# First mixture of the fused kernel: rows normalized on VectorE tile by tile ahead of their transposes, side products in the second layers

## The chip, the cores and the metric

One core of a Trainium2 chip runs the whole program. The metric is the device time of one execution in microseconds (us), as the median of several runs. A difference of 0.5% (5.3 us) is about the smallest that a measurement of this kernel can tell from none.

## The reference, cut to what matters

Three stages follow each other: a linear attention, a mixture of experts with a gate per row, and a second mixture with a capacity per expert.

```python
def _attn_ref(q, k, v, g_norm):                    # (8, 8, 576, 64) each
    kv = np.einsum('bhsd,bhse->bhde', k, v)
    out = np.einsum('bhsd,bhde->bhse', q, kv)
    rms = np.sqrt(np.mean(out * out, axis=-1, keepdims=True) + 1e-06)
    return out / rms * g_norm
def _moe_ref(x, expert_emb, tau, w1, w2):          # x (4608, 512), 8 experts, F = 1024
    logits = xn @ en.T / tau                       # xn, en: rows over their norms
    expert_idx = np.argmax(logits, axis=1)
    gate_w = probs[np.arange(N), expert_idx]       # probs: softmax of the logits
    for e in range(E):
        mask = expert_idx == e
        out[mask] = gate_w[mask, None] * (np.maximum(x[mask] @ w1[e], 0.0) @ w2[e])
def _moe2_ref(x, w_gate, w1, w2):                  # at most 576 rows an expert, best logits first
    ...
        out[mask] = np.maximum(x[mask] @ w1[e], 0.0) @ w2[e]
```

The division by `rms` and the product with `g_norm` at the end of the attention are what the change moves.

## The kernel before, in words

**The stages.** The attention loop takes the heads in 40 steps. It stores rows of 528 numbers in DRAM (`xbuf`): 512 values not yet normalized, 8 gate logits, and 8 factors 1/rms, one a head. Rows of one expert are then gathered by an index table, one tile of up to 128 rows at a time. An expert has five such tiles (`TL`), in two pieces: columns 0 to 255 and the rest (0 to 319 and the rest for expert 0). The products of a piece are laid out with the features on the partitions, so each tile is turned before it is used.

**One tile.** `gather` (L667) issues the indirect DMAs of an expert's tiles on GpSimd (L675) and then, on the same engine, `normed` for each (L661): L664 multiplies the 128 x 512 values by the row's factors and L665 by `g_norm`, in place. These two are called a pair here. `xtile` (L685) turns the tile on TensorE (L695), ScalarE writes the upper half `xh` (L697), VectorE the rest `xl` (L698), and `gate_in` (L627) reads the tile for the gates: a sum of squares on ScalarE (L630) and a copy of eight logits on GpSimd (L631). Five `xg` buffers exist.

**One expert.** Numbers are split in two for the products: `layer1` (L710) does three matmuls in place of one (L724 to L726), for a quarter f of the 1024 features and one piece c. Then ScalarE writes `hh` (L732) and VectorE `hl` (L733) out of PSUM. `layer2_t` (L742) does the second layer in two halves `dp`, with L763 to L765, and ScalarE copies the result to `yT` (L773). `rows_out` (L817) turns the results back, ScalarE scales them by the gate `gts` into `yr` (L790), VectorE copies the row index beside them (L791), and `rows_l` makes the logits of the second mixture (L810 to L814). PSUM has two buffers for products (`mm`) and two for turned tiles (`tp`).

**Weights.** `wcast` (L566) takes the next 128 x 1024 block: ScalarE's L578 writes `whi`, VectorE's L584 the rest `wlo` from the raw block, and SP then issues a further load into one of three raw buffers (L562).

**Gates and side products.** `gates(e)` is a generator of small VectorE operations on 128 x 5 and 128 x 40 (L639 to L656); `next` runs a part, `run_gen` the rest. `w2g_ops` (L833) makes a product of two weight matrices that the last experts use: ScalarE lays out `wgB` (`big`, L854), and then 128 VectorE operations L861 on 128 x 512, one for each call of `aside`.

**The order of the work** is the order in which this code is written: each engine has one queue and takes its instructions in that order, SP and GpSimd for their DMAs too. `ASIDE` says how many asides stand in each of five places of an expert's loop, and `XT0` the steps of the last attention group at which expert 0's first three tiles are turned. Expert 0 is written out by hand (L1070 to L1091), experts 1 to 5 are a loop (L1423), experts 6 and 7 follow by hand. In expert 0's second piece, expert 1's tiles are gathered; in each loop those of the next expert. The loop before:

```python
            for c in range(2):
                layer1(0, e, f, c)
                aside(ASIDE[0])
                if f > 1:
                    next(gt, None)
...
                if f < 2 or 2 * (f - 2) + c < 3:
                    wcast()
            if f == 1:
                gather(0, e + 1)
        wcast()
        layer2_t(e, 0, 0)
        xtiles(0, e + 1, 0, 1)
        aside(ASIDE[1])
        layer2_t(e, 0, 1)
        xtiles(0, e + 1, 1, 3)
        aside(ASIDE[2])
```

Of the kernel before, what the change touches and what calls it, by code (L numbers as in the profile page):

```python
# [36 lines left out]

NWARM = (18, 28, 6)

ASIDE = (1, 5, 5, 5, 3)  # L40

EARLY = 0

# [18 lines left out]

NYR = 4

XT0 = (5, 6, 8)

ROWS = (4.4, 2.8, 1.6)

# [12 lines left out]
def fused_kernel(ctx, tc, q, k, v, g_norm, emb, tau, w1, w2, wgate, v1, v2, out):  # L81
    nc = tc.nc
    V = nc.vector
# [16 lines left out]
    early = ExitStack()  # L100
# [125 lines left out]
    def run_gen(g):  # L226
        for _ in g:
            pass
# [432 lines left out]
    def normed(xg, n, eng):  # L661

        x = xg[:n, :HD].rearrange("p (h d) -> p h d", h=H)
        eng.tensor_tensor(x, x, xg[:n, HD + E:XP, None].to_broadcast([n, H, D]), op=OP.mult)  # L664
        eng.tensor_tensor(x, x, gB[:n, None, :].to_broadcast([n, H, D]), op=OP.mult)  # L665

    def gather(m, e, lo=0, hi=5, early=False, eng=nc.gpsimd):  # L667
        for i, (c, t, p, n, o) in list(enumerate(TL[m, e]))[lo:hi]:
            n += p
            if early:  # L670
                xg = mk(wpB, [128, XP], F32, "xg0", bufs=2) if i < 2 else kvx[0].rearrange("p a b c w -> p (a b c w)")[:, :XP]
            else:
                xg = mk(mp, [128, XP], F32, "xg", bufs=5)
            buf, idx, wd = (xbuf[:GA * TG * 128] if early else xbuf, tabi, XP) if m == 0 else (ybuf, tab2, YP)
            nc.gpsimd.indirect_dma_start(  # L675
                out=xg[:n, :wd], out_offset=None, in_=buf[:, :],
                in_offset=bass.IndirectOffsetOnAxis(ap=idx[:n, e * SC + t:e * SC + t + 1], axis=0))
            XG[m, e, i] = xg
        if m == 0 and eng:
            for i, (c, t, p, n, o) in list(enumerate(TL[m, e]))[lo:hi]:  # L680
                normed(XG[m, e, i], p + n, eng)

    XT = {}

# [22 lines left out]
    def layer1(m, e, f, c):  # L707
        run_gen(layer1_g(m, e, f, c))
# [33 lines left out]
    def layer2_t(e, c, dp, mid=None):  # L742
        run_gen(layer2_g(e, c, dp, mid))
# [205 lines left out]
    for n, st in enumerate(steps):  # L949
        gi, u, hg = st  # L950
        i = n % len(UNITS)
        if gi + 1 < NG and i in KVAT[gi > 0]:
            bg.append(kv(2 * gi + 2 + KVAT[gi > 0].index(i)))
        if n + 2 < len(steps):
            qa(*steps[n + 2])
        if i % 2 == 0 and i < 8:
            m = 4 * gi + i // 2 + 4
            if m < 2 * B:
                load_main(m // 2, "q", m % 2)
        if i == 9 and gi + 1 < NG:  # L960
            load_tail(gi + 1, "q")
        if gi == NG - 1 and i in XT0:
            xtile(0, 0, XT0.index(i), False)
        late = qb(*st, late)
        if i == 0 and gi > 0:
            bg.append(group_end(gi - 1))
        pump()
        if n in LOADS:
            wload(LOADS[n])
        if n in CASTS and n < 30:  # L970
            wcast(1, nc.gpsimd if CASTS[n] else V, 0)
        if gi == NG - 1:
            if i == 0:
                kvs.close()
                wpB = ctx.enter_context(tc.tile_pool(name="wpB", bufs=RING // 2))
                mo0 = ExitStack()
                MP["xh1"] = MP["xl1"] = mo0.enter_context(tc.tile_pool(name="moex", bufs=1))
                WP.append(wpB)
            elif n in CASTS:
                wcast(1, nc.gpsimd if CASTS[n] else V, 1)  # L980
            if i == EARLY:
                index(0, 3)
                gather(0, 0, 0, 3, early=True, eng=None)
            if i == SCALE:
                rows0 = [XG[0, 0, t] for t in range(2)]
                for t in range(2):
                    normed(rows0[t], 128, nc.gpsimd)
            if i == SCALE + 1:
                normed(XG[0, 0, 2], CUT - 256, V)
            if i == LASTP[0]:  # L990
                ge = group_end(gi)
            if i in LASTP:
                next(ge)
        if gi == 0 and i < 4:
            pump()
# [29 lines left out]
    while bg:  # L1025
        pump()
    index(2, NCOL)
    gather(0, 0, 3, 6, eng=None)
    LSUB[0](V)
    pe(1.1)  # L1030
    LSUB[1](V)
# [2 lines left out]
    for i, us in enumerate(ROWS):  # L1034
        pe(total - us - done)
        done = total - us
        normed(XG[0, 0, 3 + i], sum(TL[0, 0][3 + i][2:4]), V)
        xtiles(0, 0, 3 + i, 4 + i)
    run_gen(f0)
    grp.close()  # L1040
# [29 lines left out]
    gt = gates(0)  # L1070
    aside(1)
    for f in range(4):
        layer1(0, 0, f, 1)
        wcast()
        aside(1)
        if f == 0:
            next(gt)
            gather(0, 1)
        elif f < 3:
            next(gt)  # L1080
        else:
            run_gen(gt)
            ro = rows_out(0, 0)
            next(ro)
            next(ro)
    layer2_t(0, 1, 0, lambda: (run_gen(ro), xtiles(0, 1, 0, 1)))
    xtiles(0, 1, 1, 2)
    aside(2)
    layer2_t(0, 1, 1, lambda: xtiles(0, 1, 2, 3))
    xtiles(0, 1, 3, 5)  # L1090
    aside(2)  # L1091

# [330 lines left out]
    for e in range(1, E - ND):  # L1423
        gt = gates(e)
        if e == 2:
            flags()
        for f in range(4):
            for c in range(2):
                layer1(0, e, f, c)
                aside(ASIDE[0])  # L1430
                if f > 1:
                    next(gt, None)
                if f == 0:
                    if c == 0:
                        ro = rows_out(e - 1, 1)
                        next(ro)
                        next(ro)
                    else:
                        run_gen(ro)
                if f < 2 or 2 * (f - 2) + c < 3:  # L1440
                    wcast()
            if f == 1:
                gather(0, e + 1)
        wcast()
        layer2_t(e, 0, 0)
        xtiles(0, e + 1, 0, 1)
        aside(ASIDE[1])
        layer2_t(e, 0, 1)
        xtiles(0, e + 1, 1, 3)
        aside(ASIDE[2])  # L1450
        layer2_t(e, 1, 0)
        run_gen(rows_out(e, 0))
        xtiles(0, e + 1, 3, 5)
        aside(ASIDE[3])
        layer2_t(e, 1, 1)
        aside(ASIDE[4])


    e6, e7 = E - 2, E - 1
    for f in range(4):  # L1460
        layer1(0, e6, f, 0)
        if f == 0:
            gt = gates(e6)
        next(gt, None)
        if f == 0:
            ro = rows_out(e6 - 1, 1)
            next(ro)
            next(ro)
        if f == 1:
            run_gen(ro)  # L1470
        wcast()
        if f == 1:
            gather(0, e7)
    run_gen(wg)
    for f in range(4):
        layer1(0, e6, f, 1)
        wcast()
        if f in (1, 2):
            xtiles(0, e7, f - 1, f)
    H7.append(mk(mp, [128, KF, CAP[E - 1]], F32, "big"))  # L1480
    layer1(0, e7, 0, 0)
    a = logits_w(e6, 0)
    xtiles(0, e7, 2, 3)
    a()
# [713 lines left out]
```

## Time and profile before

| | us |
|---|---|
| median of 3 runs (lowest, highest) | 1067.63 (1066.28, 1070.65) |
| the profiled execution: its time, its span | 1072.25, 1070.5 |
| TensorE (PE) busy | 1020.1, 95% of the span |
| VectorE (DVE) busy | 732.2, 68% |
| ScalarE (ACT) busy | 526.8, 49% |
| GpSimd (POOL) busy | 293.5, 27% |

All rows are of one execution. A busy share is a mean over the whole span, and the stages differ: the first product of expert 0 starts near 137 us, that of expert 1 near 210 us, each further expert some 60 us later, and the last copy of L773 starts at 637 us; the second mixture follows. So a stretch is read by itself. Times within the program are counted from the start of the span. `PEclk` is the share of full speed that TensorE's clock was granted.

### The profile page before, as it was taken

Reading aid. Unit: us, or ns where it says so; the run is one execution under the profiler, and the core shown is the slowest. Engines: PE = TensorE matmul, PEld = TensorE weight load, DVE = VectorE, ACT = ScalarE, POOL = GpSimd, SP = SyncE. Lnnn points to the kernel's source line nnn. Section 1 sums busy time; section 2 is a strip of 40 time slices with the busy share of each in tenths; the row PEclk is TensorE's granted clock in tenths of the full one; section 3 lists DMA queues with packets and bytes.
Section 4 is the critical chain, followed back from the end, with each engine's and each line's share of the span. In section 5 each row is a group of like instructions: output and inputs, shape, how many; then the busy total and the mean of one; then the engine's idle time right before and its main releaser. Section 6 shows DMA issues by size and latency. Waiting matters only on the chain. (4 is left out here: it accounts for less than half of the span.)

```text
span 1070.5 us, 20601 instructions
## 1 busy us (share of the span) xinstructions
PE 1020.1 (95%) x8234; PEld 939.0 (88%) x8234; DVE 732.2 (68%) x1443; ACT 526.8 (49%) x915; POOL 293.5 (27%) x389
## 2 busy tenths in 40 slices
PE   7888798889999999999999998999999999999998
PEld 7777688789999999999988987989889898989896
DVE  4467876376978778786756765668685959595860
ACT  2566724754444545353643312556565656555551
POOL 2011427241616061423400113131304131313211
PEclk8999789889999999999999999999999999999999
DMA  9999535444343525243411114434334343424211
GB/s 285 379 346 326 190 138 189 156 134 145 119 139 98 163 95 167 86 158 108 139 47 59 41 47 141 149 109 157 120 129 159 110 148 118 149 99 152 106 55 45
DMA packets 94679, 152.46 MB, mean 142 GB/s; under 512 B 11321, under 2 KB 52281, under 8 KB 94579
## 3 DMA queue, kind: packets, MB, share of 16 engines
q1 hardware_dynamic: 85011, 121.65, 34.2%
q0 software_dynamic: 9040, 28.93, 8.4%
q8 instruction: 65, 1.06, 0.4%
q10 hardware_dynamic: 528, 0.52, 0.2%
q14 instruction: 35, 0.29, 0.1%
HBM read 121.26 MB, written 29.82 MB: 141 GB/s over the span
## 5 line engine op out<-in xcount | busy, mean ns | idle before, releaser
L724 PE MATMUL mm<-xh,whi 128*128 128x256 f32 (+7 forms) x512 | 156.2, 305 | 6.5 <-DVE hl L733 6.1
L763 PE MATMUL mm<-hh,whi 128*128 128x256 f32 (+7 forms) x512 | 156.4, 305 | 1.7 <-ACT hh L732 1.7
L725 PE MATMUL mm<-xl,whi 128*128 128x256 f32 (+7 forms) x512 | 153.2, 299 | 2.0 <-DVE xl L698 2.0
L726 PE MATMUL mm<-xh,wlo 128*128 128x256 f32 (+7 forms) x512 | 153.2, 299 | 0.0
L764 PE MATMUL mm<-hl,whi 128*128 128x256 f32 (+7 forms) x512 | 151.9, 297 | 1.0 <-DVE hl L1546 0.6
L765 PE MATMUL mm<-hh,wlo 128*128 128x256 f32 (+7 forms) x512 | 151.5, 296 | 0.0
L861 DVE SCALAR_TENSOR_TENSOR rc<-xg,big 128x512 bf16<-128x512 f32 x128 | 110.7, 865 | 2.6
L584 DVE TENSOR_TENSOR wlo<-wraw,whi 128x1024 fp32r<-128x1024 f32 x72 | 91.1, 1269 | 22.5 <-ACT whi L578 21.9
L724 PEld LDWEIGHTS mm<-xh,whi 128*128 128x128 f32 x512 | 98.2, 192 | 8.7 <-DVE hl L733 7.2
L725 PEld LDWEIGHTS mm<-xl,whi 128*128 128x128 f32 x512 | 98.3, 192 | 2.2 <-DVE xl L698 2.2
L763 PEld LDWEIGHTS mm<-hh,whi 128*128 128x128 f32 x512 | 96.9, 189 | 3.8 <-ACT hh L732 2.0
L726 PEld LDWEIGHTS mm<-xh,wlo 128*128 128x128 f32 x512 | 98.2, 192 | 0.0
L764 PEld LDWEIGHTS mm<-hl,whi 128*128 128x128 f32 x512 | 96.9, 189 | 1.4 <-DVE hl L1546 0.8
L765 PEld LDWEIGHTS mm<-hh,wlo 128*128 128x128 f32 x512 | 96.8, 189 | 0.0
L773 ACT COPY yT<-mm 128x512 f32<-128x512 f32 (+7 forms) x31 | 19.9, 643 | 149.9 <-PE mm L765 149.9
L675 POOL DMA_INDIRECT xg<-xbuf,tabi x40 | 43.5, 1088 | 171.8 <-ACT sj L630 74.9
L2097 POOL DMA_INDIRECT out<-tm,ti x40 | 43.7, 1092 | 160.2 <-ACT tm L2095 140.5
L578 ACT CAST whi<-wraw 128x1024 fp32r<-128x1024 f32 x72 | 74.9, 1044 | 0.4 <-DMA wraw<-in_moe_w 0.3
L732 ACT ACTIVATE hh<-mm 128x512 fp32r<-128x512 f32 (+7 forms) x56 | 36.8, 658 | 74.8 <-PE mm L726 72.1
L1840 DVE TENSOR_TENSOR wlo<-wraw,whi 128x1024 fp32r<-128x1024 f32 (+1 forms) x63 | 61.0, 987 | 11.6 <-ACT whi L1843 11.6
L665 POOL TENSOR_TENSOR xg<-xg,gB 128x512 f32<-128x512 f32 (+6 forms) x37 | 61.0, 1649 | 2.9
L733 DVE SCALAR_TENSOR_TENSOR hl<-mm,hh 128x512 fp32r<-128x512 f32 (+7 forms) x56 | 42.6, 760 | 21.6 <-ACT hh L732 21.5
(363 smaller groups left out, 2687.9 us busy)
## 6 DMA issues: line engine op xcount, KB each, us to landing
wraw<-in_moe_w SPq DMA_DIRECT2D x127, 512.0 KB, 3.9
kmain<-in_k SPq DMA_DIRECT2D x16, 576.0 KB, 8.7
vmain<-in_v SPq DMA_DIRECT2D x16, 576.0 KB, 11.0
xbuf<-xo SPq DMA_DIRECT2D x16, 528.0 KB, 11.5
qmain<-in_q SPq DMA_DIRECT2D x16, 512.0 KB, 9.8
ybuf<-yr SPq DMA_DIRECT2D x31, 260.0 KB, 2.1
xg<-in_moe_w SPq DMA_DIRECT2D x16, 256.0 KB
xg<-in_moe_w_gate SPq DMA_DIRECT2D x8, 256.0 KB, 3.8
```

Source lines behind the costliest of these rows:

```text
L578: nc.scalar.copy(hi, raw)
L584: eng.tensor_tensor(lo, raw, hi.bitcast(F32), op=OP.subtract)
L665: eng.tensor_tensor(x, x, gB[:n, None, :].to_broadcast([n, H, D]), op=OP.mult)
L724: nc.tensor.matmul(o, a, xh[:, kd, :N], start=(kd == 0), stop=False)
L725: nc.tensor.matmul(o, a, xl[:, kd, :N], start=False, stop=False)
L726: nc.tensor.matmul(o, b, xh[:, kd, :N], start=False, stop=(kd == KD - 1))
L763: nc.tensor.matmul(o, a, hh[:, kf, :N], start=(kf == 0), stop=False)
L764: nc.tensor.matmul(o, a, hl[:, kf, :N], start=False, stop=False)
L765: nc.tensor.matmul(o, b, hh[:, kf, :N], start=False, stop=(kf == KF - 1))
L861: V.scalar_tensor_tensor(junk, raws[i], 1.0, wgB[:, x], op0=OP.mult, op1=OP.mult, accum_out=w2g[:, i // KF, i % KF, x:x + 1])
L1840: V.tensor_tensor(l, x, h.bitcast(F32), op=OP.subtract)
L2097: st_ = nc.gpsimd.indirect_dma_start(out=out, out_offset=bass.IndirectOffsetOnAxis(ap=TI[e, t][:n, :1], axis=0), in_=yo[:n], in_offset=Non ...
```

## The change

- The pairs of experts 1 to 7 (35 tiles) leave `gather` and GpSimd. `gather` puts each tile into a queue `NQ`, and `norm(k)` runs `normed` on VectorE for the next k tiles; the calls stand one by one where the tile is wanted later. Expert 0's last three tiles were on VectorE before and now go by the same queue; its first two stay on GpSimd.
- In experts 1 to 5, the pairs stand after both products of the fourth quarter, after `layer2_t(e, 0, 0)` and its transposes, and two after `layer2_t(e, 0, 1)`. The aside after each product of the fourth quarter is left out; `ASIDE` has one more in each of two later places, so that a loop still has 26.
- Expert 0's second piece: the gates are finished ahead of the fourth quarter's product, and the logits and the first tile of `rows_out` come ahead of the last weight cast and aside there, not behind them.
- The third tile of expert 0 is turned one step of the attention loop earlier (`XT0`).

Below lines of the changed file are shifted: 664 and 665 are the same, L698 is L703, L733 is L738, L791 is L796, L675 is L681, L861 is L866.

```diff
-ASIDE = (1, 5, 5, 5, 3)
+ASIDE = (1, 5, 6, 6, 3)
...
-XT0 = (5, 6, 8)
+XT0 = (5, 6, 7)
...
-    def gather(m, e, lo=0, hi=5, early=False, eng=nc.gpsimd):
+    NQ = []
+
+    def norm(k=1):
+        for _ in range(k):
+            normed(*NQ.pop(0), V)
+
+    def gather(m, e, lo=0, hi=5, early=False):
...
             XG[m, e, i] = xg
-        if m == 0 and eng:
-            for i, (c, t, p, n, o) in list(enumerate(TL[m, e]))[lo:hi]:
-                normed(XG[m, e, i], p + n, eng)
+            if m == 0 and not early:
+                NQ.append((xg, n))
...
     gt = gates(0)
     aside(1)
     for f in range(4):
+        if f == 3:
+            run_gen(gt)
         layer1(0, 0, f, 1)
+        if f == 3:
+            ro = rows_out(0, 0)
+            next(ro)
+            next(ro)
         wcast()
         aside(1)
         if f == 0:
...
         elif f < 3:
             next(gt)
-        else:
-            run_gen(gt)
-            ro = rows_out(0, 0)
-            next(ro)
-            next(ro)
-    layer2_t(0, 1, 0, lambda: (run_gen(ro), xtiles(0, 1, 0, 1)))
+        if f > 1:
+            norm()
+    layer2_t(0, 1, 0, lambda: (run_gen(ro), xtiles(0, 1, 0, 1), norm()))
     xtiles(0, 1, 1, 2)
+    norm()
     aside(2)
-    layer2_t(0, 1, 1, lambda: xtiles(0, 1, 2, 3))
+    layer2_t(0, 1, 1, lambda: (norm(), xtiles(0, 1, 2, 3)))
...
                 layer1(0, e, f, c)
-                aside(ASIDE[0])
+                if f < 3:
+                    aside(ASIDE[0])
...
                     wcast()
+                if f == 3:
+                    norm()
             if f == 1:
                 gather(0, e + 1)
         wcast()
         layer2_t(e, 0, 0)
         xtiles(0, e + 1, 0, 1)
+        norm()
         aside(ASIDE[1])
         layer2_t(e, 0, 1)
+        norm(2)
         xtiles(0, e + 1, 1, 3)
...
             gather(0, e7)
+    norm()
     run_gen(wg)
     for f in range(4):
         layer1(0, e6, f, 1)
         wcast()
+        if f != 1:
+            norm()
         if f in (1, 2):
             xtiles(0, e7, f - 1, f)
...
     layer1(0, e7, 0, 0)
+    norm()
```

How this moves instructions, engine by engine (name of what is written, `<-` what is read, and the shape):

VectorE, expert 0's second piece, from the third quarter's `wlo` to the first row indices of `rows_out`, before:

```order
L584 TENSOR_TENSOR wlo_2617<-wraw_2328,whi_2616 128x1024
L649 TENSOR_SCALAR gw_2524<-gw_2524 128x5
L650 RECIPROCAL gw_2524<-gw_2524 128x5
L651 TENSOR_TENSOR gx_2528<-gx_2528,gw_2524 128x40
L733 SCALAR_TENSOR_TENSOR hl0_2487<-mm_2629,hh0_2486 128x576
L584 TENSOR_TENSOR wlo_2657<-wraw_2519,whi_2656 128x1024
L654 TENSOR_REDUCE gts_180<-gx_2528 128x5
L655 TENSOR_SCALAR gts_180<-gts_180 128x5
L656 RECIPROCAL gts_180<-gts_180 128x5
L791 COPY yr_2680<-tabi_178 128x8
L791 COPY yr_2689<-tabi_178 128x8
```

and in the change (`hl0_2487` of L738 is the last quarter's, as that of L733 above):

```order
L584 TENSOR_TENSOR wlo_2607<-wraw_2328,whi_2606 128x1024
L649 TENSOR_SCALAR gw_2524<-gw_2524 128x5
L650 RECIPROCAL gw_2524<-gw_2524 128x5
L651 TENSOR_TENSOR gx_2528<-gx_2528,gw_2524 128x40
L664 TENSOR_TENSOR xg_2530<-xg_2530 128x512
L665 TENSOR_TENSOR xg_2530<-xg_2530,gB_96 128x512
L654 TENSOR_REDUCE gts_180<-gx_2528 128x5
L655 TENSOR_SCALAR gts_180<-gts_180 128x5
L656 RECIPROCAL gts_180<-gts_180 128x5
L738 SCALAR_TENSOR_TENSOR hl0_2487<-mm_2624,hh0_2486 128x576
L796 COPY yr_2663<-tabi_178 128x8
L796 COPY yr_2672<-tabi_178 128x8
```

A pair of expert 1's first tile and the three operations that finish the gates now stand ahead of the last `hl`; the last `wlo` has gone from behind that `hl` to behind the two row indices.

VectorE, end of expert 1's first layer and start of its second (`xg_3088` to `xg_3092` are expert 2's tiles), before:

```order
L584 TENSOR_TENSOR wlo_3218<-wraw_3086,whi_3217 128x1024
L733 SCALAR_TENSOR_TENSOR hl1_2960<-mm_3223,hh1_2959 128x2x280
L861 SCALAR_TENSOR_TENSOR rc_2483,w2g_2482<-xg0_2926,big_2481 128x512
L654 TENSOR_REDUCE gts_180<-gx_3140 128x5
L655 TENSOR_SCALAR gts_180<-gts_180 128x5
L656 RECIPROCAL gts_180<-gts_180 128x5
L584 TENSOR_TENSOR wlo_3255<-wraw_3146,whi_3254 128x1024
L698 TENSOR_TENSOR xl0_3312<-tp_3313,xh0_3311 128x4x128
L861 SCALAR_TENSOR_TENSOR rc_2483,w2g_2482<-xg0_2926,big_2481 128x512
```

and in the change:

```order
L584 TENSOR_TENSOR wlo_3207<-wraw_3086,whi_3206 128x1024
L664 TENSOR_TENSOR xg_3088<-xg_3088 128x512
L665 TENSOR_TENSOR xg_3088<-xg_3088,gB_96 128x512
L738 SCALAR_TENSOR_TENSOR hl1_2960<-mm_3214,hh1_2959 128x2x280
L654 TENSOR_REDUCE gts_180<-gx_3130 128x5
L655 TENSOR_SCALAR gts_180<-gts_180 128x5
L656 RECIPROCAL gts_180<-gts_180 128x5
L664 TENSOR_TENSOR xg_3090<-xg_3090 128x512
L665 TENSOR_TENSOR xg_3090<-xg_3090,gB_96 128x512
L584 TENSOR_TENSOR wlo_3247<-wraw_3136,whi_3246 128x1024
L703 TENSOR_TENSOR xl0_3304<-tp_3305,xh0_3303 128x4x128
L664 TENSOR_TENSOR xg_3092<-xg_3092 128x512
```

The first tile's pair stands ahead of the last `hl`, the second ahead of the last `wlo`, and the aside L861 behind that `hl` is gone.

GpSimd, the gather of expert 2, before:

```order
L675 DMA xg_3094<-xbuf_71,tabi_178 128x528
L675 DMA xg_3096<-xbuf_71,tabi_178 80x528
L664 TENSOR_TENSOR xg_3088<-xg_3088 128x512
L665 TENSOR_TENSOR xg_3088<-xg_3088,gB_96 128x512
L664 TENSOR_TENSOR xg_3090<-xg_3090 128x512
```

and in the change:

```order
L681 DMA xg_3094<-xbuf_71,tabi_178 128x528
L681 DMA xg_3096<-xbuf_71,tabi_178 80x528
L631 COPY gvl_181<-xg_3088 128x8
L631 COPY gvl_181<-xg_3090 128x8
L631 COPY gvl_181<-xg_3092 128x8
```

The ten operations of the five pairs are gone from behind the DMAs, and the copies of the logits follow at once.

## Rows read from the trace of the kernel before

**Rows 1.** Table of stretches: us, PE, PEld, DVE, ACT, POOL busy, clock, DMA share, GB/s.

```profile
250.00:550.00 300.00, 298.40 (x2310) 286.66 (x2309) 227.43 (x492) 142.53 (x243) 105.48 (x100) 1.00 0.39 126
```

**Rows 2.** TensorE's waits, 176 to 300 us: total, times, longest, in us.

```profile
PE mm L724 <- DVE hl L733: 6.1, 3, 4.8
PE mm L763 <- ACT hh L732: 1.7, 1, 1.7
PE tp L784 <- ACT yr L790: 1.6, 1, 1.6
PE mm L764 <- DVE hl L733: 0.4, 1, 0.4
```

**Rows 3.** Table of stretches, columns as in rows 1.

```profile
160.00:190.00 30.00, 27.24 (x201) 25.59 (x200) 18.98 (x31) 13.48 (x22) 22.95 (x30) 1.00 0.57 181
193.30:200.00 6.70, 5.07 (x23) 4.57 (x23) 2.97 (x14) 4.10 (x8) 0.55 (x1) 0.50 0.68 231
229.30:234.20 4.90, 4.81 (x22) 4.81 (x23) 4.18 (x8) 0.00 (x0) 0.00 (x0) 0.50 0.67 218
234.20:240.00 5.80, 5.80 (x49) 5.80 (x48) 3.80 (x9) 4.52 (x6) 0.69 (x5) 1.00 0.27 91
```

**Rows 4.** VectorE by line, 177 to 189 us: busy us, mean ns, idle before.

```profile
L584 DVE TENSOR_TENSOR wlo<-wraw,whi 128x1024 fp32r<-128x1024 f32 x3 | 5.4, 1794 | 0.2 <-ACT whi L578 0.2
L643 DVE TENSOR_TENSOR gx<-gvl,gw 128x40 f32<-128x40 f32 x1 | 1.3, 1260 | 0.0
L646 DVE TENSOR_TENSOR gw<-gvn,gw 128x5 f32<-128x5 f32 x1 | 1.0, 1045 | 0.0
```

**Rows 5.** One line's instructions, whole run: min/median/max ns, first and last start.

```profile
L861 DVE SCALAR_TENSOR_TENSOR rc<-xg,big x128: 671/691/1861, 221.0 to 508.8; 128x512 bf16<-128x512 f32 x128
L584 DVE TENSOR_TENSOR wlo<-wraw,whi x72: 1199/1222/2111, 98.7 to 682.6; 128x1024 fp32r<-128x1024 f32 x72
L813 DVE TENSOR_TENSOR lr<-lr,gts x26: 153/174/1242, 197.3 to 578.8; 128x16 f32<-128x16 f32 x15, 64x8 f32<-64x8 f32 x3, 24x8 f32<-24x8 f32 x2, 128x8 f32<-128x8 f32 x1
L733 DVE SCALAR_TENSOR_TENSOR hl<-mm,hh x56: 668/740/874, 145.2 to 538.6; 128x512 fp32r<-128x512 f32 x24, 128x640 fp32r<-128x640 f32 x8, 128x576 fp32r<-128x576 f32 x4, 128x560 fp32r<-128x560 f32 x4
L665 DVE TENSOR_TENSOR xg<-xg,gB x3: 686/691/745, 162.3 to 169.4; 128x512 f32<-128x512 f32 x2, 96x512 f32<-96x512 f32 x1
```

**Rows 6.** VectorE by line, 217 to 229 us, columns as in rows 4.

```profile
L584 DVE TENSOR_TENSOR wlo<-wraw,whi 128x1024 fp32r<-128x1024 f32 x2 | 3.3, 1647 | 1.2 <-ACT whi L578 1.2
L813 DVE TENSOR_TENSOR lr<-lr,gts 128x8 f32<-128x8 f32 (+2 forms) x3 | 2.5, 834 | 0.1
L791 DVE COPY yr<-tabi 128x8 int32<-128x8 int32 (+2 forms) x3 | 1.8, 613 | 0.0
L814 DVE TENSOR_TENSOR L<-lr,vneg 128x8 f32<-128x8 f32 (+2 forms) x3 | 1.3, 429 | 0.1
L861 DVE SCALAR_TENSOR_TENSOR rc<-xg,big 128x512 bf16<-128x512 f32 x1 | 1.1, 1134 | 0.0
```

**Rows 7.** GpSimd by line, 213.5 to 226.9 us.

```profile
L665 POOL TENSOR_TENSOR xg<-xg,gB 128x512 f32<-128x512 f32 (+1 forms) x5 | 7.3, 1463 | 0.4
L664 POOL TENSOR_TENSOR xg<-xg 128x512 f32<-128x512 f32 (+1 forms) x5 | 5.7, 1136 | 0.0
```

**Rows 8.** GpSimd by line, 250 to 550 us.

```profile
L675 POOL DMA_INDIRECT xg<-xbuf,tabi x25 | 28.1, 1125 | 139.6 <-ACT xh L697 62.3 <-ACT sj L630 59.2 <-issue 18.2
```

**Rows 9.** ScalarE in order of time: start, us, then the idle time before.

```profile
188.45 1.21 ACT L854 COPY big<-xg 128x512 f32<-128x512 f32 x1 [2.09 <-DMA xg<-in_moe_w_gate]
```

**Rows 10.** VectorE by line, 250 to 550 us.

```profile
L861 DVE SCALAR_TENSOR_TENSOR rc<-xg,big 128x512 bf16<-128x512 f32 x121 | 105.5, 871 | 2.6
L698 DVE TENSOR_TENSOR xl<-tp,xh 128x512 fp32r<-128x512 f32 (+5 forms) x28 | 18.3, 653 | 28.0 <-ACT xh L697 28.0
```

**Rows 11.** TensorE and VectorE in order of time, near 137 us.

```profile
137.01 0.63 PE L725 MATMUL mm<-xl,whi 128*128 128x320 f32 x1 [2.02 <-DVE xl L698]
...
136.09 0.53 DVE L522 TENSOR_TENSOR oh<-iob,sf 128x360 bf16<-128x360 bf16 x1
```

More of the change, by code (lines that the diff above doesn't have):

```diff
@@ L982, in fused_kernel @@
                 index(0, 3)
-                gather(0, 0, 0, 3, early=True, eng=None)
+                gather(0, 0, 0, 3, early=True)
             if i == SCALE:
@@ L1027, in fused_kernel @@
     index(2, NCOL)
-    gather(0, 0, 3, 6, eng=None)
+    gather(0, 0, 3, 6)
     LSUB[0](V)
@@ L1036, in fused_kernel @@
         done = total - us
-        normed(XG[0, 0, 3 + i], sum(TL[0, 0][3 + i][2:4]), V)
+        norm()
         xtiles(0, 0, 3 + i, 4 + i)
@@ L1481, in fused_kernel @@
     layer1(0, e7, 0, 0)
+    norm()
     a = logits_w(e6, 0)
```

## The prediction

> **What bounds the kernel now.** I read the table of stretches first. From 250 to 550 us, where most of the loops of experts 1 to 5 run and 25 of the 35 moved tiles are gathered, TensorE is busy 298.4 of 300 us at the full clock and VectorE 227 of 300 [rows 1]. Whatever leaves or joins another engine there can give back 1.6 us at most; it can only cost, if VectorE becomes late. So I looked for places where TensorE does wait. The list of its waits from 176 to 300 us, where expert 0 ends and expert 1 runs, has 6.1 us for `hl` on VectorE in three waits, the longest 4.8 (it ends at 229.4 us), 0.4 for the same tile under another line, 1.7 for `hh` and 1.6 for `yr` on ScalarE: 9.8 us [rows 2]. The waits between 190 and 197 us and the one that ends at 229.4 are each followed by a stretch in which the granted clock is 0.50, that is 1.2 in place of 2.4 GHz: 193.3 to 200 and 229.3 to 234.2 us. Shorter waits need not bring that: from 160 to 190 us TensorE is busy 27.2 of 30 us and the clock is 1.00 throughout [rows 3].
>
> Next, why VectorE is late there. From 177 to 189 us its small operations last six times as long as elsewhere: the five-element L646 takes 1.0 us, the forty-element L643 1.26, against a median of 0.17 for the small L813; three `wlo` take 1.79 each, against 1.22 [rows 4, 5]. From 217 to 229 us it is the same [rows 6]. Both stretches are those in which GpSimd runs its pairs L664 and L665, five tiles each time; the second string lies between 213.5 and 226.9 us [rows 7]. Operations that read SBUF twice are the ones stretched most clearly: L861 takes 671 ns at least, 691 as a median and 1861 at most; `hl`, which reads PSUM, never passes 874 over all its widths [rows 5]. I read it as the two engines holding each other up in SBUF, one instruction at a time.
>
> **The change, part by part.**
>
> (a) Pairs off GpSimd. 35 tiles lose L664 and L665 there (1.1 and 1.5 us each [rows 7]). What stands behind them on GpSimd is not in a hurry: from 250 to 550 us it sat idle for 140 us ahead of its gathers [rows 8]. By itself this part is worth 0. What counts is that the stretching of VectorE ends.
>
> In the stretch before 229.4 us it makes: two L584 of mean 1647 against 1222, 0.85; three L813 by 0.66 and three L791 by 0.45 over 0.17, 3.3; three L814 by 0.26, 0.8; one L861 by 0.44: 5.4 us [rows 5, 6]. They all stand in one queue ahead of the `hl` that TensorE waits 4.8 us for. 5.4 us earlier, it would wait for almost nothing; but not all of VectorE's string hangs together (1.2 us of it waits for ScalarE's `whi`). Bounds: 0 to 1.5 us of the wait left. I take 0.6: **-4.2**.
>
> In the stretch from 177: three L584 by 0.57, L643 by 1.09, L646 by 0.87 and two more of five elements, taken as the same length, 1.7: 5.4 us [rows 4, 5]. It reaches TensorE over two legs. SP's queue issues the next weight load only when L584 has read the raw buffer, the load of the gate weights is queued behind it, ScalarE's copy L854 waits for that (2.1 us at 188.45), and `hh` stands behind L854 [rows 9]. The other leg is `gts`, which the `yr` copies need. Against it stands one new pair, which the change puts ahead of `gts` and of the last `hl`: 2 x 0.69 = 1.4 us [rows 5]. That leaves 4.0 us, against waits of 9.8 - 4.8 - 0.7 (the third `hl` wait, (d)) = 4.3. Bounds: 0.2 to 2 us left. I take 0.9: **-3.4**.
>
> (b) The clock. [...] At full clock 49 matmuls take 5.8 us, 0.118 each; the second stretch has 22 in 4.9 us, 2.6 at full clock; the first has 5.07 busy us, half of that at full clock [rows 3]: 2.3 + 2.5 = 4.8 us. Bounds: 0 and 4.8. I take 4.4, near the end that 160 to 190 us is like: **-4.4**.
>
> (c) The pairs on VectorE in experts 1 to 5. From 250 to 550 us 25 pairs of 1.4 us come in, 35 us. The stretching that leaves is, in L861 alone, 121 x (871 - 691) ns = 22 us [rows 5, 10], and more in the smaller ones. So VectorE is at most 13 us in 300 busier, at 240 of 300, and not late on average. Where the pairs stand: two in the last quarter of each first layer, around the last `hl`; one after the first call of the second layer; two after its second call. In the first layer a slot of VectorE holds `hl` (0.7), some gates, L584 (1.2) and now a pair (1.4), some 3.7 us, against 2.8 us of TensorE (24 matmuls of 0.118); the aside (0.7) has left that slot, and the next slot has no L584. So `hl` is late by about 1 us, while the next product runs ahead into the other PSUM buffer. Every tile is normalized at least one product (2.8 us or more) before its transposes. Bounds: 0 to 1 us for each of five loops. I take the low end, 0.1 each, as the nearest row, the same loops with VectorE stretched, has TensorE at 298.4 of 300: **+0.5**. That cover gone, each pair ahead of an `hl` costs its 1.4 us.
>
> Against moving work between these two engines speaks a caution in the Trainium skill (Perfetto Trace Analysis, section Optimizing Scalar/DVE Operations): GpSimd and VectorE share an SBUF read port, so it might not help. By it (a), (b) and (d) would fall away and the sum would be about 0; by the rows, what GpSimd keeps in these loops are gathers and short copies, and the sum below stands. The trace decides for the rows: L813 has a median of 0.17 us and the long ones lie beside the pairs.
>
> (d) The third wait for `hl`, 6.1 - 4.8 less 0.5 at 182.5 us, is 0.7 us at 288 us [rows 2]; it follows the pairs of the next gather in the same manner: **-0.7**.
>
> (e) The asides that moved (26 in a loop before and after) go from the last first-layer slots into the second layers, where VectorE waits for ScalarE's `xh`, 28 us from 250 to 550 us [rows 10]. That idle time covers them: 0. Without it, two asides of 0.7 us a loop would cost 1.4.
>
> (f) The third tile of expert 0 is turned one step sooner in the attention loop, so its `xl` moves ahead of L522 (0.53 us) and one reduction; TensorE waited 2.02 us for it [rows 11]. At most -1.2; the transposes now stand ahead of a product that could go at once, so at worst +1. I take the near end, as the wait is there now and longer than what is moved: **-1.0**.
>
> (g) Expert 7's tiles: five pairs, in expert 6's slots and ahead of expert 7's first product, where the asides have run out. Bounds 0 to 2, like (c): **+0.2**.
>
> Sum: -4.2 - 3.4 - 4.4 + 0.5 - 0.7 - 1.0 + 0.2 = -13.0 us, from the profiled execution's 1072.25 to 1059.2. That execution lies 4.6 us above the median of the runs, 1067.63; nothing in the places above accounts for these 4.6, so I take the sum from the median: **1054.6 us**.
>
> **The rivals.**
>
> (1) The waits go but the clock still falls, since a wait of a microsecond or so is left in each place. Term (b) is lost: 1059.0 us. For: two such waits remain in the sum. Against: 160 to 190 us [rows 3].
>
> (2) The change does nothing in the end: the stretching has another cause, or, as the caution above has it, passes over to the pairs and their new neighbours. Then only (f) stays: about 1066.5 us. For: L791, which reads one tile, is stretched as well, so two reads of SBUF are not the whole story. Against: the pairs that VectorE itself runs while GpSimd has none took a flat 0.69 us an operation [rows 5].
>
> (3) Slower: VectorE becomes the bound at the end of the first layer. Two pairs, 2.8 us, stand around the last two `hl`, which the second layer reads; if the stretching stays, VectorE is at 262 of 300 us, each of five loops waits up to 2.8 us, and expert 0, whose waits then stay, 1.4 more. With half of the five, 7 + 1.4 - 1.0 = +7.4: 1075 us. It decides as soon as L861 stays above some 0.8 us on average, for then the 22 us of (c) are not given back. For: the queue is in order and 76% busy already [rows 1]. Against: the rows of (a).
>
> **How the numbers follow.** The forecast has a chance of 0.68, rival (1) 0.17, (2) 0.09, (3) 0.06. With every bound at its good end the time is 1050; with those of (a), (c) and (g) at their bad ends 1063, rival (1) among them. The range is 1049 to 1063 and leaves out (2) and (3). A measurement of this kernel tells about 0.5%, 5.3 us, from no change, so faster means under 1062.3: nearly all of the forecast and (1), and none of the rest, 0.84; same 0.10; slower 0.06.
>
> **What would show it.** Right: the profile of the changed kernel has no pair on GpSimd after expert 0's two early tiles, L813 and L646 near 0.17 us everywhere, L861 at a mean near 0.7, TensorE's waits in the places of [rows 2] near 2 us in place of 9.8, and clock 1.00 from about 150 us on. From 250 to 550 us TensorE stays at 298. Wrong: a half-speed stretch near 195 or 225 us (rival 1), L861 still near 0.87 (rivals 2 and 3), or a wait of TensorE for `hl` or for a tile's pair once a loop (rival 3, or the upper bound of (c)). The prediction falls if the time is above 1063.

## The result and the profile after

The changed kernel takes 1055.6 us (median of 5 runs, 1053.09 to 1056.0), the kernel before 1069.18 in the same comparison (1066.28 to 1070.65). The ratio is 0.9872, 95% interval 0.9852 to 0.9893: 1.3% or 13.6 us faster. The forecast was 1054.6. The profiled execution took 1055.79 us with a span of 1054.0, against 1072.25 and 1070.5 before: between the two traces lie 16.5 us, more than between the medians, since the profiled execution before lies 3.1 us above its median and the one after 0.2.

What TensorE waits for from 176 to 300 us, after (total, times, longest, in us), against the 9.8 us of [rows 2]:

```profile
PE mm L769 <- DVE hl L738: 0.4, 1, 0.4
PE mm L768 <- ACT hh L737: 0.3, 1, 0.3
```

The table of stretches (columns as in [rows 1]) for the place of the two half-speed stretches of [rows 3] and for the loops:

```profile
190.00:235.00 45.00, 45.00 (x369) 44.13 (x368) 33.55 (x76) 32.35 (x52) 5.46 (x10) 1.00 0.54 175
250.00:550.00 300.00, 298.09 (x2319) 286.37 (x2318) 230.26 (x558) 143.14 (x240) 27.97 (x49) 1.00 0.37 119
233.90:533.30 299.40, 297.94 (x2310) 286.56 (x2309) 232.15 (x553) 143.04 (x243) 29.50 (x50) 1.00 0.39 126
```

TensorE is busy without a gap from 190 to 235 us, at clock 1.00. From 250 to 550 us VectorE carries 66 operations more, 50 of them the 25 pairs, and is busy 230.26 us in place of 227.43 [rows 1]. The changed kernel is 16 us further in its work by then; the last row holds the same 2310 matmuls as that of before, and there VectorE is busy 232.15 us, 4.7 more. Why so little, the view of single lines shows (min/median/max ns; L866, L818 and L796 are L861, L813 and L791 of before):

```profile
L866 DVE SCALAR_TENSOR_TENSOR rc<-xg,big x128: 672/691/704, 211.2 to 490.2; 128x512 bf16<-128x512 f32 x128
L818 DVE TENSOR_TENSOR lr<-lr,gts x26: 153/174/178, 192.2 to 562.1; 128x16 f32<-128x16 f32 x15, 64x8 f32<-64x8 f32 x3, 24x8 f32<-24x8 f32 x2, 128x8 f32<-128x8 f32 x1
L796 DVE COPY yr<-tabi x31: 154/164/169, 187.7 to 500.9; 128x8 int32<-128x8 int32 x23, 64x8 int32<-64x8 int32 x2, 96x8 int32<-96x8 int32 x1, 24x8 int32<-24x8 int32 x1
L584 DVE TENSOR_TENSOR wlo<-wraw,whi x72: 1199/1222/1228, 98.8 to 666.1; 128x1024 fp32r<-128x1024 f32 x72
L665 DVE TENSOR_TENSOR xg<-xg,gB x38: 678/691/749, 160.0 to 524.9; 128x512 f32<-128x512 f32 x30, 24x512 f32<-24x512 f32 x2, 96x512 f32<-96x512 f32 x1, 80x512 f32<-80x512 f32 x1
```

The longest L866 takes 704 ns where it was 1861, the longest L818 178 where it was 1242 [rows 5]: none of these lines is stretched any more.

Where the 16.5 us come from shows if the start of each matmul is set against that of the same matmul in the trace of before. The difference grows by so much in each stretch (us of before's span, negative is earlier; the first 126 us, in which the attention loads its data, are left out, see the end):

```
                        126-146 146-205 205-244 244-300 300-550  550-end   sum
the change               -2.1    -6.5    -7.2    -1.2    +0.7    +0.2   -16.1
e1 pairs on GpSimd       -1.1    -2.8    -5.2    -1.1    +3.6    +0.2    -6.4
e2 idle products         -3.0    -3.0    -3.2    -0.7    +3.7    +0.5    -5.7
e3 before, order alone   +0.7    -4.9    -0.8    -0.1     0.0    -0.1    -5.3
e4 before, lump on DVE   -0.1    +0.9     0.0    +4.7   +24.4    +2.3   +32.1
e5 lump on GpSimd        -3.2    -2.0    -0.8    +0.4    +0.8    +0.1    -4.7
e6 order back            -1.2    -1.2    -7.1    -1.3    +0.7    +0.5    -9.5
e7 third tile back        0.0    -6.7    -7.2    -1.2    +0.7    +0.5   -14.0
e8 two more moves        -1.4    -4.0    -7.1    -1.2    -0.5    +0.5   -13.7
e9 and other DMA queue   -1.1    -8.3    -5.1    -1.3    -0.5    +0.7   -15.5
e10 idle copies          -3.2    -5.6    -6.6    -1.2    +0.7    +0.7   -15.2
e11 pairs doubled        -2.1    -4.0    -3.4    +3.8   +13.3    +0.3    +8.0
e12 side products back   -3.2    -2.3    -7.2    -0.7    +0.7    +0.2   -12.6
```

Each row is one profile. All are set against the one trace of before; still the sums lie within 2.6 us of the differences of the medians. The column 126-146 ranges from -1.1 to -3.2 among the ten kernels that have the third tile of the change (mean -2.2) and from -0.1 to +0.7 among the three that have the old one; 146-205 ranges from -2.3 to -6.7 among kernels that are alike there (the change, e7, e12); the column 205-244 repeats within 0.1 where nothing was done to it.

### The profile page after: what moved, and what is told of

Its sections match the earlier page's. It is cut to its first block, busy times and chain, and to the rows that moved or that the text cites. A ratio compares the mean times of both kernels' runs of the same rounds, so it can differ in the third digit from the quotient of the medians.

```text
span 1054.0 us, 20601 instructions
## 1 busy us (share of the span) xinstructions
PE 1014.1 (96%) x8234; PEld 933.3 (89%) x8234; DVE 732.1 (69%) x1513; ACT 526.6 (50%) x915; POOL 191.8 (18%) x319
## 5 line engine op out<-in xcount | busy, mean ns | idle before, releaser
L584 DVE TENSOR_TENSOR wlo<-wraw,whi 128x1024 fp32r<-128x1024 f32 x72 | 87.7, 1221 | 30.6 <-ACT whi L578 30.4
L866 DVE SCALAR_TENSOR_TENSOR rc<-xg,big 128x512 bf16<-128x512 f32 x128 | 88.1, 688 | 2.9
L578 ACT CAST whi<-wraw 128x1024 fp32r<-128x1024 f32 x72 | 75.0, 1044 | 0.4 <-DMA wraw<-in_moe_w 0.4
L681 POOL DMA_INDIRECT xg<-xbuf,tabi x40 | 41.4, 1034 | 176.1 <-ACT sj L630 79.4
L738 DVE SCALAR_TENSOR_TENSOR hl<-mm,hh 128x512 fp32r<-128x512 f32 (+7 forms) x56 | 42.7, 762 | 36.8 <-ACT hh L737 36.3
L2100 PE MATMUL mA<-whi,hx 128*128 128x512 f32 x136 | 56.6, 416 | 0.0
```

Source lines behind the costliest of these rows:

```text
L578: nc.scalar.copy(hi, raw)
L584: eng.tensor_tensor(lo, raw, hi.bitcast(F32), op=OP.subtract)
L866: V.scalar_tensor_tensor(junk, raws[i], 1.0, wgB[:, x], op0=OP.mult, op1=OP.mult, accum_out=w2g[:, i // KF, i % KF, x:x + 1])
L2100: nc.tensor.matmul(ps[:, x_, :], hh, a, start=(kf == 0), stop=False)
```

## The experiments

Theory: the strings of pairs on GpSimd stretched VectorE's operations, and an `hl` that TensorE waits for stood behind them. Rivals: the new order in expert 0's second piece brings the gain, not the engine; or VectorE has room for the pairs wherever they stand.

**The engine, with the order kept (e1, e5).**

```diff
-            normed(*NQ.pop(0), V)
+            normed(*NQ.pop(0), nc.gpsimd)
```

(expert 0's tiles stay on VectorE)

> The changed kernel with all its new places, but the pairs of experts 1 to 7 are given to GpSimd again. Theory (the pairs on GpSimd stretch VectorE's operations): GpSimd is at some 290 us busy again, the mean of the side product L866 goes from 688 back to some 870 ns, and of the 14 us that lie in experts 0 and 1 two thirds or more are lost: 1063 to 1068 us. Rival (the new order of expert 0's second piece, of the side products and of the third tile brings the gain, not the engine): 1054 to 1057 us.

Measured: 1062.44 us, ratio 0.9933 (0.9909 to 0.9957). About half of the gain is lost, a little less than expected, and not where the theory said: the wait near 229 us did not come back (-5.2 in 205-244, 2.0 less than the change). From 300 us on 2.9 us are lost, and 3.7 in 146-205, which is within the spread there. GpSimd in order of time (start, us, then the idle time before) tells why:

```profile
214.14 1.30 POOL L665 TENSOR_TENSOR xg<-xg,gB 128x512 f32<-128x512 f32 x1
227.29 0.19 POOL L631 COPY gvl<-xg 128x8 f32<-128x8 f32 x1 [11.85 <-DVE gx L643]
227.44 1.04 POOL L664 TENSOR_TENSOR xg<-xg 128x512 f32<-128x512 f32 x1
228.56 2.16 POOL L665 TENSOR_TENSOR xg<-xg,gB 128x512 f32<-128x512 f32 x1
```

With the places of the change, the copies L631 of the logits stand between the pairs, and the first of them waits 11.85 us until VectorE's gates have read the old ones. So the string of ten is cut, and three of the pairs run after the `hl` in question. The run moved the pairs in time as well as between engines. Hence e5, which gives GpSimd the five pairs at the gather, as before, with everything else as in the change:

```diff
             if m == 0 and not early:
                 NQ.append((xg, n))
+        if m == 0 and e > 0:
+            while NQ:
+                normed(*NQ.pop(0), nc.gpsimd)
```

> The changed kernel with all its new places, but the five pairs of each gather of experts 1 to 7 go to GpSimd at the gather, in one string as in the kernel before. Theory (such a string ahead of an hl is what makes VectorE late): counted from 122 us of the span on, only what the third tile (2.1 us) and the new order of expert 0's second piece (about 5) give is left of the 16.1, the wait of 4 to 5 us for hl near 229 us is back with its half-speed stretch, and the ratio to the kernel before is 0.992 to 0.995. Rival (GpSimd's share is small, the order gives most): no wait over 2 us there, ratio 0.986 to 0.989.

Measured: 1063.43 us, 0.9953 (0.9935 to 0.9971), just above the range expected. The wait is back in full (TensorE in order of time, then VectorE by line from 211 to 223 us, busy us and mean ns):

```profile
222.91 0.58 PE L732 MATMUL mm<-xh,whi 128*128 128x256 f32 x1 [4.83 <-DVE hl L741]
```

```profile
L584 DVE TENSOR_TENSOR wlo<-wraw,whi 128x1024 fp32r<-128x1024 f32 x2 | 3.3, 1644 | 1.2 <-ACT whi L578 1.2
L821 DVE TENSOR_TENSOR lr<-lr,gts 128x8 f32<-128x8 f32 (+2 forms) x3 | 2.5, 835 | 0.1
L799 DVE COPY yr<-tabi 96x8 int32<-96x8 int32 x1 | 1.0, 997 | 0.0
```

4.83 us for `hl`, behind the same 1644 and 835 ns as in [rows 6]. In 205-244 it keeps 0.8 of the 7.2 us. This settles that stretch: a string of pairs on GpSimd ahead of that `hl` costs 6.4 us, wait and clock together. From 300 us on the same strings cost nothing (+0.8 against +0.7). In 146-205 only 2.0 us are left, not the 5 expected of the order; see e3 and e6.

**Work on GpSimd that nobody reads (e2, e10).** Behind each gather of the change, 27 products of two operands, or 27 copies of one:

```diff
+        if m == 0 and e > 0:
+            for i in range(27):
+                nc.gpsimd.tensor_tensor(scr.rearrange("p (h d) -> p h d", h=3), ident[:, None, :64].to_broadcast([128, 3, 64]),
+                                        gB[:, None, :].to_broadcast([128, 3, 64]), op=OP.mult)
```

> The changed kernel, and behind each gather of experts 1 to 7 GpSimd also does 27 products of 128 x 192 (two operands in SBUF, some 13 us a gather) into a scratch tile that nobody reads. Theory (GpSimd's reads and writes hold VectorE up): nothing waits for these products, yet the mean of L866 rises to 850 ns or more, the waits for hl and the half-speed stretches come back, and the time is 1064 to 1085 us. Rival (the gain came from order or from taking a dependency off GpSimd): 1054 to 1058 us.

> As the run with 27 GpSimd products a gather that nobody reads, but with 27 copies of 128 x 192 (one operand in SBUF) in their place. Theory (two operands on GpSimd are what VectorE is held up by): VectorE's small operations stay near 0.17 us, and from 122 us on 14 to 16 of the 16.1 us stay. Rival (any work of GpSimd in SBUF stretches VectorE): only 5 to 10 stay, as with the products (5.7).

Measured: the products 1062.16 us, 0.994 (0.9916 to 0.9963), the copies 1054.57 us, 0.9867 (0.984 to 0.9894). The products took 23 to 27 us a gather, not 13. First the string of products on GpSimd, then three lines of VectorE with the products, then two with the copies (min/median/max ns):

```profile
166.46 23.10 POOL L690 TENSOR_TENSOR scr<-ident,gB 128x192 f32<-128x192 f32 x27
L801 DVE COPY yr<-tabi x31: 157/165/606, 184.1 to 505.4; 128x8 int32<-128x8 int32 x23, 64x8 int32<-64x8 int32 x2, 96x8 int32<-96x8 int32 x1, 24x8 int32<-24x8 int32 x1
L871 DVE SCALAR_TENSOR_TENSOR rc<-xg,big x128: 673/692/1414, 209.7 to 495.4; 128x512 bf16<-128x512 f32 x128
L823 DVE TENSOR_TENSOR lr<-lr,gts x26: 153/214/551, 189.7 to 567.7; 128x16 f32<-128x16 f32 x15, 64x8 f32<-64x8 f32 x3, 24x8 f32<-24x8 f32 x2, 128x8 f32<-128x8 f32 x1
```

```profile
L800 DVE COPY yr<-tabi x31: 156/165/321, 185.1 to 499.1; 128x8 int32<-128x8 int32 x23, 64x8 int32<-64x8 int32 x2, 96x8 int32<-96x8 int32 x1, 24x8 int32<-24x8 int32 x1
L870 DVE SCALAR_TENSOR_TENSOR rc<-xg,big x128: 670/691/918, 208.6 to 488.5; 128x512 bf16<-128x512 f32 x128
```

Nothing reads these products, and still they take 10.4 of the 16.1 us (7.5 of 13.6 by the medians). GpSimd's copies of the logits and its next gathers do stand behind them, but from 165 to 560 us the trace has no wait of VectorE or TensorE for GpSimd or for a gather. So it is not a dependency or the order: GpSimd's work itself holds VectorE up. The sizes expected were too high (L871 has a mean of 789 ns, not 850). The copies cost 0.9 us by the shift, which is within its spread. That does not show that one operand is harmless: L800 still reaches 321 ns against 169, and a copy is also shorter (503 ns on average from 165 to 300 us, against 846 for the products and 1136 and 1463 for the pairs [rows 7]). The longest `yr` index copy falls with them: 1283 ns before, 606, 321. Whether operands or length decide is left open.

**The order in expert 0's second piece (e3, e6).** e3 is the kernel before with this edit alone, e6 the change without it:

```diff
+        if f == 3:
+            run_gen(gt)
         layer1(0, 0, f, 1)
+        if f == 3:
+            ro = rows_out(0, 0)
+            next(ro)
+            next(ro)
         wcast()
...
-        else:
-            run_gen(gt)
-            ro = rows_out(0, 0)
-            next(ro)
-            next(ro)
```

> The kernel before, with one part of the change alone: in expert 0's second piece the gates are finished ahead of the fourth quarter and the first rows are turned ahead of the last weight cast and side product. Pairs stay on GpSimd. Theory (stretching): the stretch from 213 us is untouched, at most the 1.7 us for hh and the 1.6 us for yr near 195 us move: ratio 0.996 to 1.001. Rival (order): 0.992 or less.

> The changed kernel, but in expert 0's second piece the gates' end and the first turned rows stand again behind the fourth quarter's product, weight cast and side product. Theory (the order gives the part near 195 us by itself, since gts is ready in time for the yr copies): the wait for yr and the half-speed stretch after it come back, 3 to 5 us, ratio 0.990 to 0.993. Rival (with the stretching gone, VectorE is early enough in either order): under 1 us, ratio 0.986 to 0.989.

Measured: e3 1065.58 us, 0.9976 (0.9955 to 0.9996); e6 1057.69 us, 0.9893 (0.987 to 0.9916). The ratio of e3 lies in the theory's range, a gain of 2.7 us by the medians; that of e6 lies between the two, and its interval overlaps the change's. In the traces, in 146-205, the order alone gives 4.9 us, and without it the change keeps 1.2 of its 6.5. These sizes are of single traces: e5 has the same order, with the pairs on GpSimd as in e3, and gives 2.0 there. In both TensorE waits for `hh` near 188 us (1.81 us in e3, 1.67 in e5), but in e5 the clock is 0.76 from 186 to 193 us, in e3 1.00. What repeats is the wait for `yr`: 1.6 us before and 2.74 in e6, none with the new order in e3, e5 and the change. ScalarE in order of time, before, e3, then e6 (L859 is L854 of before, L795 the `yr` copy), then e6's TensorE:

```profile
194.58 1.27 ACT L790 ACTIVATE yr<-tp,gts 128x512 f32<-128x512 f32 x2 [0.33 <-DVE yr L791]
```

```profile
189.56 0.42 ACT L826 COPY lgT<-sm 128x320 f32<-128x320 f32 x1
189.87 1.27 ACT L790 ACTIVATE yr<-tp,gts 128x512 f32<-128x512 f32 x2
191.03 1.05 ACT L578 CAST whi<-wraw 128x1024 fp32r<-128x1024 f32 x1
```

```profile
186.29 1.04 ACT L578 CAST whi<-wraw 128x1024 fp32r<-128x1024 f32 x1
188.82 1.12 ACT L859 COPY big<-xg 128x512 f32<-128x512 f32 x1 [1.49 <-DMA xg<-in_moe_w_gate]
190.16 1.27 ACT L795 ACTIVATE yr<-tp,gts 128x512 f32<-128x512 f32 x2
```

```profile
190.90 1.06 PE L789 MATMUL tp<-ident,yT 128*64 128x128 f32 x4 [2.74 <-ACT yr L795]
```

In the old order ScalarE's queue holds the weight cast L578 and the copy L859, which waits 1.49 us for its DMA, ahead of the `yr` copies; TensorE waits 2.74 us for them and has clock 0.50 from 190 to 196 us. In the new order `lgT` and `yr` go first, and the wait and the half-speed stretch are gone, in e3 as in the change. The expectation named `gts`; the queue of ScalarE is as much of it: in e6 `yr` begins without a wait for VectorE; in the kernel before it waits 0.33 us for VectorE's index copies, which follow `gts`.

**The third tile (e7)**, `XT0 = (5, 6, 8)`:

> The changed kernel with the third tile of expert 0 turned at the old step. Theory: between 122 and 143 us the wait for xl of 2.0 us in place of 0.7 is back, and the clock comes up later, 2.1 us in all; nothing else changes, ratio 0.988 to 0.990. Rival (only the wait, 1.0 us as predicted, or nothing): 0.986 to 0.988.

Measured: 1054.91 us, 0.9875 (0.9852 to 0.9898): the whole time can't tell it from the change. In the trace the wait is back:

```profile
135.59 0.63 PE L730 MATMUL mm<-xl,whi 128*128 128x320 f32 x1 [1.97 <-DVE xl L703]
```

```profile
135.34 0.63 PE L730 MATMUL mm<-xl,whi 128*128 128x320 f32 x1 [0.66 <-DVE xl L703]
```

1.97 against 0.66 us, and from 133 to 146 us the clock is 0.74 against the change's 0.87. The stretch 126-146 gives 0.0 in place of 2.1.

**The place on VectorE (e4, e11).** e4 is the kernel before with `eng=V` in `gather`: five pairs in one lump. e11 doubles the cost of each pair:

```diff
+            for _ in range(2 if twice else 0):
+                V.tensor_tensor(xg[:n, :HD], xg[:n, :HD], xg[:n, :HD], op=OP.max)
```

> The kernel before, with the five pairs of a gather on VectorE, but all at once at the place of the gather and not tile by tile. Theory: the stretching ends as in the change, but 7 us of pairs stand in one piece ahead of an hl, against 2.8 us of TensorE's work, so each of the seven gathers makes TensorE wait some 3 to 6 us: 1073 to 1100 us. Rival (VectorE's idle time covers the pairs wherever they stand): 1054 to 1058 us.

> The changed kernel, with every pair of experts 1 to 7 followed by two further VectorE operations of the same size on the same tile (the maximum of the tile with itself, which leaves it as it is). Theory (VectorE has little room at the end of a first layer): two places a loop hold 5.1 us of VectorE's work against 2.8 us of TensorE's, 4.6 more, of which the second PSUM buffer covers 2.8: some 1.8 us a loop, 5 to 14 us in all over the change. Rival (VectorE has room for twice the pairs): under 2 us over the change.

Measured: e4 1100.29 us, 1.0293 (1.0264 to 1.0323); e11 1075.62 us, 1.0064 (1.0043 to 1.0086), 20 us over the change. TensorE's waits in e4 from 170 to 560 us, and in e11 from 250 to 530:

```profile
PE mm L724 <- DVE hl L733: 31.7, 7, 5.5
```

```profile
PE tp L792 <- DVE xl L706: 6.4, 5, 2.3
```

Seven lumps cost seven waits for `hl`, 31.7 us. In e11 the size was missed and so was the place: not `hl`, but `xl`. Two doubled pairs (5.5 us) stand ahead of the `xl` that empties the buffers for turned tiles, and the next transposes wait for those:

```profile
252.02 1.42 DVE L674 TENSOR_TENSOR xg<-xg 128x512 f32<-128x512 f32 x2
254.79 1.41 DVE L674 TENSOR_TENSOR xg<-xg 80x512 f32<-80x512 f32 x2
256.12 1.28 DVE L706 TENSOR_TENSOR xl<-tp,xh 128x512 fp32r<-128x512 f32 x2
```

A further wait of 3.1 us for `xl` stands at 542 us, in expert 6, where the change waits 0.8.

**The side products (e12)**, back behind both products of the fourth quarter:

> The changed kernel, with the side products back behind both products of the fourth quarter. Theory (as predicted, their place costs nothing): within 1 us of the change from 122 us on. Rival (pair, wlo and side product together make hl late): 0.7 to 1.4 us a loop, 4 to 7 us.

Measured: 1053.98 us, 0.9859 (0.9831 to 0.9886). In the loops it is within 0.6 us of the change, as predicted. The 4.2 us that its trace lacks in 146-205 lie in expert 0, where it is the same as the change: there ScalarE's L859 waited 2.29 us for its DMA (0.72 in the change), and TensorE 1.81 for `hh`.

```profile
183.96 1.22 ACT L859 COPY big<-xg 128x512 f32<-128x512 f32 x1 [2.29 <-DMA xg<-in_moe_w_gate]
```

**Two more moves (e8, e9).** The waits left in the change point at them: 0.8 us in expert 6, where a pair stands ahead of the `xl` of the tile before, and near 165 us 1.4 us for L665, then 0.8 for which the profile names no releaser.

```diff
-        if f != 1:
+        if f in (0, 3):
             norm()
         if f in (1, 2):
             xtiles(0, e7, f - 1, f)
+        if f == 2:
+            norm()
...
-        norm()
+        norm(2 if i == 0 else 1 if i == 1 else 0)
         xtiles(0, 0, 3 + i, 4 + i)
```

> The changed kernel with two moves: in expert 6's second piece the third quarter's pair goes behind the transposes and xl of the tile before it (TensorE waits 0.8 us there), and of expert 0's last three tiles the second and third are normalized one step earlier, while VectorE waits for ScalarE's xh (TensorE waits 1.4 and 0.8 us there). Theory (VectorE's order is what TensorE waits for): 1 to 4 us faster than the change, ratio 0.983 to 0.987, no wait for xg on L665 over 0.5 us. Rival (the tiles' DMAs land too late for an earlier pair, which then blocks VectorE): 0.987 or more.

e9 has these and, besides, `nc.scalar.dma_start` in place of `nc.sync.dma_start` for the gate weights:

> The kernel of the run before (both moves), and the loads of the gate weights for the side product are issued by ScalarE, that reads them, in place of SP, where they stand behind weight loads that wait for VectorE. Theory (in that run TensorE's waits moved to hh, behind ScalarE's copy of these weights, 1.8 us at 187 us and 0.9 for hl at 178): both go, from 122 us on 18 to 21 us are gained against the kernel before (16.1 by the change), ratio 0.980 to 0.985. Rival (the issue holds ScalarE up, or the next wait stands right behind): 0.985 to 0.988.

Measured: e8 1054.05 us, 0.9856 (0.983 to 0.9883); e9 1052.9 us, 0.9853 (0.9823 to 0.9883). Both intervals overlap the change's: neither is shown to be faster, and e9 just missed its range. The two waits went (by the shift 1.9 us near 165, 1.1 in 300-550), but in e8 expert 0 then ran into the next limit:

```profile
184.10 1.22 ACT L859 COPY big<-xg 128x512 f32<-128x512 f32 x1 [3.26 <-DMA xg<-in_moe_w_gate]
```

```profile
187.46 0.40 PE L768 MATMUL mm<-hh,whi 128*128 128x288 f32 x1 [1.83 <-ACT hh L737]
```

L859 waits 3.26 us for the gate weights, whose load stands on SP's queue behind a weight load. With ScalarE's own queue this wait is gone in e9 (-8.3 in 146-205), and 0.8 us for `yr` and 0.8 for `hl` appear in expert 1 (-5.1 in place of -7.2).

## Why the prediction held, step by step

- **The reading (GpSimd stretches VectorE)** is right: e2 shows it with work that nobody reads, e5 with the pairs themselves. By the caution that the prediction weighed (the Trainium skill, Perfetto Trace Analysis, section Optimizing Scalar/DVE Operations) the sum would have been about 0; the time fell by 1.3%.
- **(a), the wait that ends at 229.4 us**, forecast -4.2: the wait is gone entirely, -5.0 by the shift. The stretched durations, summed to 5.4 us, cover the 4.8 us of the wait, and in e5 both come back.
- **(a), the second place**, forecast -3.4 with a pair ahead of `hl` charged at 1.4: the size is about right (3.9 of the 6.5 us of the whole place, the rest is clock), but the reason is at least in part another, so the size is in part luck. The new order alone gives 4.9 of the 6.5 in e3 and 2.0 in e5, and without it 1.2 is left (e6). The prediction charged the new pair and gave the order no term: it read that `hh` stands behind L854 in ScalarE's queue, but not that `yr` stood there behind a cast and that copy. How much is the order's and how much the stretching's stays open: kernels that are alike there differ by 4.4 us.
- **(b), the clock**, -4.4: both half-speed stretches are gone: by the shift 4.1 us from 194 to 202 us, less the 1.6 of the `yr` wait, and 2.1 from 229 to 236, together 4.6. Rival (1) is out. It stood on the waits falling away, which they did.
- **(c), 25 pairs in the loops**, +0.5: 0.1 us earlier from 300 to 519 us, so 0. VectorE's load rose by 2.8 us in 300, by 4.7 over the same matmuls, against 13 as an upper bound. What covers the pairs is used up at twice their cost (e11), and first at the transposes, of which the prediction said only that a tile is ready in time.
- **(d)** -0.7: -1.2. **(e)** 0: within 0.6 us in the loops (e12).
- **(f), the third tile**, -1.0: -2.1 (the mean of the ten traces with this tile is -2.2). The term was mis-sized, since it held the wait alone. The clock was low there too (0.74 in 133 to 146 us) and comes up sooner.
- **(g), expert 7's tiles**, +0.2: +0.7. The bound of 2 held; the pair ahead of `xl` in expert 6 costs it, as e8 shows.
- **The sum** was -13.0, the traces have -16.1 from 126 us on, the medians -13.6. The choice to take the sum from the median and not from the profiled execution is what brought the forecast to within 1 us. That it is so near is in part luck: the terms were 3.1 us short of the traces, which are set against an execution 3.1 us above its median. The stated bounds at their good ends add up to -15.6, which gives 1052.0 and not the 1050 written; it decides nothing.
- **Rival (3)** did not come, but its mechanism is real: with the same pairs in another place (e4) or of twice the length (e11) VectorE is the bound, at +32 and +6 us over the kernel before.

Left open in the prediction was why L791, which reads one tile, is stretched. The trace of before sorts the operations (min/median/max ns):

```profile
L791 DVE COPY yr<-tabi x31: 130/166/1283, 194.4 to 519.5; 128x8 int32<-128x8 int32 x23, 64x8 int32<-64x8 int32 x2, 96x8 int32<-96x8 int32 x1, 24x8 int32<-24x8 int32 x1
L638 DVE TENSOR_SCALAR gw<-gvn x8: 163/169/1005, 179.4 to 560.1; 128x5 f32<-128x5 f32 x8
L810 DVE TENSOR_REDUCE lr<-sm x26: 171/208/227, 197.1 to 578.6; 128x16 f32<-128x64 f32 x15, 64x8 f32<-64x32 f32 x3, 24x8 f32<-24x32 f32 x2, 128x8 f32<-128x32 f32 x1
```

L813 (two operands in SBUF), the copy L791 and L638 (a tensor_scalar, up to 1005 ns) are stretched to about the length of one GpSimd operation, the reduction L810 (at most 227 ns) and `hl` (at most 874) are not. The Trainium skill (SBUF — State Buffer, section Who interferes with whom) says the same: an operation with two SBUF inputs contends with a GpSimd instruction that reads SBUF, a copy or tensor_scalar can in a mode with two ports, a tensor_reduce never, and the one that comes second waits for the whole instruction. The trace agrees in which are stretched and how far; whether L791 and L638 ran in such a mode no run here shows.

## What to carry to other kernels

If small operations of VectorE take several times their median, look at what GpSimd runs beside them; moving that work to VectorE can pay although VectorE is the busier engine, as its own load hardly rises. Then the place decides: the same pairs gave 13.6 us tile by tile and cost 32 in a lump, so a string of them should not stand ahead of the `hl` or `xl` that TensorE waits for next. Read the queues of the other engines at that place too: in expert 0 a part of the gain hung on the order in ScalarE's queue.

## What the runs showed that was not expected

- Much of the spread between profiles is made early. Up to 126 us of the span, profiles of kernels with the same code there differ from the trace of before by -4.3 (e9) to +1.0 us (e1); after 550 us all but e4 add 0.7 at most. A difference of 2 us in expert 0 is seen in the shift of the traces and not in the whole time (e7).
- Waits alike are not followed by the same clock. In e3 TensorE waited 1.81 us for `hh` at 189.7 us and had clock 1.00 from 186 to 198 us; in e12 it waited 1.81 us in the same place and had 0.86 and 0.85 from 184 to 196 us. In e5 it was 1.67 us and 0.76. What else counts was not looked for.
- A copy of eight logits cut a string of pairs in two (e1): it waited 11.85 us on VectorE's gates and so held GpSimd's queue, which kept the pairs out of the way of the critical `hl`.
